# Slot tables by one-hot products instead of scatters, and a new order of splits, gathers and loads

## The chip, the cores and the metric

The kernel runs on one core of a Trainium2 chip. The metric is device time of one execution in microseconds (us). The engines are TensorE (PE; its weight loads are listed as PEld), VectorE (DVE), ScalarE (ACT), GpSimd (POOL) and SyncE (SP), which issues most DMA transfers. Each engine runs its own instructions in order.

## The reference

Three stages follow one another on 4 batches of 1152 positions, 8 heads of 64.

1. Attention: queries are averaged in pairs (576 per batch); scores against all 1152 keys, softmax, product with V. Its output, transposed, is x: 2304 rows of 512.
2. A routed expert layer: rows with `x @ w_skip > 0` go to the best of 8 experts by `x @ w_gate`, are sent through `relu(xc @ w1[e]) @ w2[e]`, scaled by the gate's probability and added to x. The other rows pass unchanged.
3. A dense layer on all rows: `((x @ w1) * (x @ w2)) @ w3 @ w_out`, with 512 to 1024 to 1024 to 512 columns.

```python
skip_score = x @ w_skip
do_compute = skip_score > 0
e_idx = np.argmax(logits, axis=1)
h = np.maximum(xc[mask] @ w1[e], 0.0)
y[mask] = gate_w[mask, None] * (h @ w2[e])
out[do_compute] = xc + y
...
h = a * b @ w3
return (h @ w_out).astype(np.float32)
```

The weights of stage 3 arrive as 64-bit floats and are converted to 32 bits on the chip.

## The kernel before

Matrix products in fp32 are made of pieces of type fp32r: a value is split into a high and a low part (names end in h and l), and three products of the parts are added. Splitting is work for ACT (the high part, a cast) and DVE or POOL (the low part, a subtraction).

**Attention** is a loop over 144 steps (16 head pairs, `p`, of 9 query tiles, `l`) and 7 more to drain it. Its order is written by hand: in step `i` PE transposes the exponentials of step i-2 (L289), multiplies some of them with V (L325) and makes the scores of step i (L255). DVE takes the maximum (L266) and a third of the copies out of PSUM, ACT the exponentials and the other copies (L308). POOL prepares the K and Q of later head pairs (`prep`, L208, L209, in two phases of steps) from raw buffers that SP loads. Beside this, two generators are advanced by `side`:

- `conv_ops` converts the stage-3 weights in 40 chunks: SP loads a chunk, POOL squares its high words (L82), DVE makes four operations of it (L96, L97, L101, L104), SP stores it to DRAM (L105). It is advanced from step 8 on.
- `route_ops` runs once per batch, 44 steps after the batch's first: logits, the choice of expert, and the position of each row among the rows of its expert (products with a triangle of ones). Ten indirect DMAs of POOL (`put`, L417) then scatter the row numbers into two tables in DRAM: `tab` (rows ordered by expert) and `perm` (skipped rows in front, then the others). Its letters say what comes next: "P" is PE work, which `side` does only in steps where a PSUM bank is free, "D" is DVE work, "C" the scatters. At the end it transposes five blocks of x (L448), scales them into the row buffers `XR` (L451; four buffers, block 4 uses buffer 0 again) and has SP store them to `x_d` in DRAM (L456).

**Transition.** The last batch's route runs after attention. As a filler for PE, the product W' = w3 @ w_out is made in eight blocks of 24 matmuls (`wprime`, L513). Its operand, the third weight, comes in blocks of 128 columns (`RW`, two buffers) and is split by ACT (L554), DVE and POOL (L555, L556). `emit_meta` computes on one partition which expert each tile of 128 rows has. Then SP loads the order vector and three index columns from DRAM (L823, L587) and the first expert's weights, POOL gathers rows from `x_d` (`gather`, `ld_x`), and `split` splits the weights.

**Expert loop.** Up to 25 tiles of 128 rows, each in a runtime `If` nested in the one before; 11 run with these inputs. Each tile: `xg @ W1`, relu, transposes, `@ W2`, and a scatter of the rows back to `x_d`. When the expert changes, weights are split and the next ones loaded.

**Dense stage.** Six groups of 384 rows, fetched by the order vector: products with m1 and m2 (L883), their product, and the product with W' (L513). Its first steps split m1 and m2 into the buffers of the expert weights (`split_cols`, L865, L866).

## Time and profile before

| | |
|---|---|
| median of 3 runs | 1099.67 us (1098.1 to 1102.2) |
| profiled execution | 1107.73 us, span of its records 1105.6 us |
| mean granted clock of PE | 0.981 |
| busy share of the span | PE 93%, PEld 76%, DVE 53%, ACT 44%, POOL 36% |
| DMA | 144.92 MB |

Attention takes about half of the span, the transition from there to 632 us, the expert loop to 777 us, the dense stage the rest. Times in rows are microseconds from the start of the span. A busy PE means that its matmul records cover the time; granted clock 1.00 is 2.4 GHz, 0.50 is 1.2 GHz.

### The profile page before, as it was taken

To read this page: it belongs to the slowest core of one execution; us is meant where nothing else is said; L and a number is where in the kernel's file an instruction comes from. 1 tells how busy PE (TensorE), PEld (TensorE's weight loads), DVE (VectorE), ACT (ScalarE), POOL (GpSimd) and SP (SyncE) were. 2 spreads that over 40 slices of the span, in tenths; PEclk is the share of its full clock that TensorE was granted. 3 is DMA by queue.
4 is the path that set the end of the run, shared out by engine and by line. 5 is a ranking of instruction groups with operands and counts; after the bars stand their busy time and mean duration, and the time that the engine had idled before them with its cause. 6 is when DMAs were issued, how large, how long until landed. Compare 5 with 4: busy or idle time off the path is not lost. (4 is left out here: it accounts for less than half of the span.)

```text
span 1105.6 us, 16864 instructions
## 1 busy us (share of the span) xinstructions
PE 1031.4 (93%) x6060; PEld 834.8 (76%) x6060; DVE 583.6 (53%) x883; ACT 482.3 (44%) x903; POOL 393.7 (36%) x411
## 2 busy tenths in 40 slices
PE   5799999999999899899998699998899999999995
PEld 4577776777767677676776488786799898989894
DVE  6588888788876788775633322437531221213120
ACT  4466665666655566565521322434432221212120
POOL 4643524563544435250824623439301010110101
PEclk9899999999999999999999699999899999999998
DMA  9776787587874878527518841506101010100000
GB/s 265 193 229 195 225 234 219 117 192 218 250 223 89 186 212 251 151 66 150 163 39 125 265 168 40 188 24 240 34 10 48 14 44 20 39 33 26 29 1 31
DMA packets 73003, 144.92 MB, mean 131 GB/s; under 512 B 16576, under 2 KB 26304, under 8 KB 72898
## 3 DMA queue, kind: packets, MB, share of 16 engines
q1 hardware_dynamic: 63698, 127.79, 41.7%
q0 software_dynamic: 6080, 14.26, 4.0%
q10 hardware_dynamic: 3120, 1.57, 0.9%
q8 instruction: 53, 0.87, 0.4%
q14 instruction: 52, 0.43, 0.1%
HBM read 86.23 MB, written 22.96 MB: 99 GB/s over the span
## 5 line engine op out<-in xcount | busy, mean ns | idle before, releaser
L266 DVE TENSOR_REDUCE sm<-s 128x1 f32<-128x1152 f32 x144 | 195.3, 1356 | 117.5 <-PE s L255 91.5
L255 PE MATMUL s<-k,q 128*128 128x384 f32 x864 | 204.9, 364 | 29.4 <-DVE pt L308 17.3
L255 PEld LDWEIGHTS s<-k,q 128*128 128x128 f32 x864 | 147.2, 192 | 98.1 <-issue 46.9
L308 ACT COPY pt<-s 128x384 f32<-128x384 f32 x288 | 137.6, 479 | 179.9 <-PE s L289 173.9
L278 ACT ACTIVATE p<-s,sm 128x1152 f32<-128x1152 f32 x144 | 176.3, 1224 | 16.6 <-DVE sm L266 16.1
L325 PE MATMUL vb<-pt,vr 128*64 128x256 f32 (+1 forms) x1152 | 170.7, 418 | 4.3 <-DVE xr L451 2.5
L289 PE MATMUL s<-cs,p 128*128 128x128 f32 x1296 | 169.7, 277 | 4.0 <-ACT p L278 3.6
L289 PEld LDWEIGHTS s<-cs,p 128*128 128x128 f32 x1296 | 151.2, 143 | 14.8 <-ACT p L278 7.5
L887 DVE TENSOR_TENSOR ar<-b,ar 128x384 f32<-128x384 f32 x48 | 26.7, 557 | 189.7 <-PE b L883 189.7
L902 POOL DMA_INDIRECT out_dram<-ar,ord x18 | 17.9, 994 | 271.0 <-ACT ar L901 266.3
L325 PEld LDWEIGHTS vb<-pt,vr 128*64 128x64 f32 x1152 | 70.2, 136 | 56.7 <-issue 22.5
L308 DVE COPY pt<-s 128x384 f32<-128x384 f32 x144 | 78.8, 547 | 2.7 <-PE s L289 1.8
L209 POOL TENSOR_TENSOR kl<-kr,kh 128x384 fp32r<-128x384 f32 x45 | 47.5, 1056 | 77.2 <-DMA k<-kl 66.6
L888 ACT CAST CVh<-ar 128x384 fp32r<-128x384 f32 x48 | 24.6, 513 | 107.7 <-DVE ar L887 107.7
L82 POOL TENSOR_TENSOR cm<-ch 128x512 f32<-128x512 f32 x40 | 42.1, 1057 | 76.1 <-DVE ca L104 47.1
L513 PE MATMUL b<-W1h,CVh 128*128 128x512 f32 x176 | 60.1, 402 | 0.7 <-issue 0.5
L513 PE MATMUL b<-W2h,CVh 128*128 128x512 f32 x176 | 60.7, 404 | 0.2
L513 PE MATMUL b<-WPh,CVh 128*128 128x512 f32 x144 | 57.4, 399 | 0.0
L513 PE MATMUL b<-WPl,CVh 128*128 128x512 f32 x144 | 56.9, 395 | 0.0
L513 PE MATMUL b<-WPh,CVl 128*128 128x512 f32 x144 | 56.8, 394 | 0.0
L901 ACT COPY ar<-b 128x512 f32<-128x512 f32 x18 | 10.6, 587 | 86.2 <-PE b L513 86.2
L208 POOL TENSOR_SCALAR kh<-kr 128x384 fp32r<-128x384 f32 x45 | 26.3, 584 | 57.9 <-PE s L255 52.1
(194 smaller groups left out, 1799.0 us busy)
## 6 DMA issues: line engine op xcount, KB each, us to landing
R<-in_w_dram SPq DMA_DIRECT2D x16, 1024.0 KB, 8.8
vr<-in_v_dram SPq DMA_DIRECT2D x16, 576.0 KB, 4.9
kr<-in_k_dram SPq DMA_DIRECT2D x15, 576.0 KB, 5.3
qr<-in_q_dram SPq DMA_DIRECT2D x15, 576.0 KB
k<-kh SPq DMA_DIRECT2D x30, 288.0 KB, 5.7
k<-kl SPq DMA_DIRECT2D x30, 288.0 KB, 15.3
q<-qnl SPq DMA_DIRECT2D x60, 144.0 KB, 4.2
ch<-in_w3t_dram SPq DMA_DIRECT2D x16, 512.0 KB, 4.8
```

Source lines behind the costliest of these rows:

```text
L82: POOL.tensor_tensor(m, hf, hf, op=ALU.mult)
L208: POOL.tensor_scalar(KH[i][:, cc], rawk[p][:, cc], 1.0, 0.0, op0=ALU.mult, op1=ALU.add)
L209: POOL.tensor_tensor(KL[:, cc], rawk[p][:, cc], f(KH[i][:, cc]), op=ALU.subtract)
L255: m = PE.matmul(sp[:, c, 0:384], lhsT=lt, rhs=kk[:, 384 * c:384 * c + 384], start=(n == 0), stop=(n == len(seq) - 1))
L266: DVE.tensor_reduce(sm, sp[:, :, 0:384], axis=AX.XY, op=ALU.max, negate=True)
L278: ACT.activation(pt, sp[:, :, 0:384], AF.Exp, bias=sm, scale=1.0, accum_out=SM[b][:, hp, c:c + 1])
L289: m = PE.transpose(tp[:, u * 128:u * 128 + 128], src[:, kt * 128:kt * 128 + 128], ident)
L308: m = (DVE.tensor_copy(o, i_) if eng is DVE else ACT.copy(o, i_)).ins
L325: PE.matmul(acc[64 * h:64 * h + 64, 0:n], lhsT=vr[:, h, kt, :], rhs=pt[:, kt, h, :], start=(kt == 0), stop=(kt == KT - 1))
L513: PE.matmul(o, lhsT=lh[a], rhs=rh[b_], start=(first and n == 0), stop=(last and n == len(order) - 1))
L887: DVE.tensor_tensor(cv, pb[:, 0:GT], av, op=ALU.mult)
L888: ACT.copy(CV[0][:, c], cv)
```

## The change

- **Tables in SBUF.** The scatters and the DRAM tables go. The index of a row is divided into a low part (7 bits, the partition of its slot) and a high part (the column). For each block of 128 rows two one-hot matrices are built by comparison with an `iota` row: 128 columns for the low part, and 146 (`tab`) plus 18 (`perm`) columns for the high part, these multiplied by row number plus one. A matmul of the two puts every row number into its slot, and DVE adds the result to `slots`. In the first three batches POOL builds, into two buffers, and the matmuls of each block are a "P" of their own; in the last batch DVE builds all five blocks, and ten matmuls in a row add them up. Empty slots are then set to an index out of bounds. The index column of a tile is copied from SBUF; the order vector needs no load.
- **Third weight.** The converted third weight is stored in blocks of columns, so that an `RW` block is one run of 4 KB in each partition; there are three `RW` buffers, loaded further ahead by SP, and DVE alone makes the low parts in `wprime`.
- **Buffers.** Five row buffers instead of four, one raw K buffer instead of two (the second raw K of the start uses `KL`), the temporaries of `emit_meta` in a part of `WPr`.
- **Order.** The conversion starts earlier: its first squares at step 4, its further steps from step 6. The index copies come before the first load of W1. `gather(1)` comes before `ld_x(0)`. The transposes of the first dense group (`x2_first`) move into tile 0, m2's load behind W2's next load. m1's split moves into the `Else` arm of each nested `If`, where it runs once, when the tiles have ended; m2's split stays behind the loop.

```diff
+    def c_src(name, c):
+        if name == "w3t":
+            return wsrc[name].rearrange("(a p f) t -> p a f t", p=128, f=F)[:, c % 8, CW * (c // 8):CW * (c // 8) + CW, :]
+        return wsrc[name].rearrange("(p n) t -> p n t", p=128)[:, c * CW:(c + 1) * CW, :]
+
+    def c_dst(name, c, t):
+        if name == "w3t":
+            u, a = 4 * (c // 8), c % 8
+            SP.dma_start(wd[name].rearrange("(u p a f) -> p u a f", u=8, p=128, f=128)[:, u:u + 4, a],
+                         t.rearrange("p (u f) -> p u f", u=4))
+        else:
+            SP.dma_start(wd[name].rearrange("(p n) -> p n", p=128)[:, c * CW:(c + 1) * CW], t)
...
         ms = [sq(nxt[0]), sq(nxt[1])]
+        yield
...
-    XR = [keep.tile([128, XW], F32, name=f"xr{i}") for i in range(4)]
+    XR = [keep.tile([128, XW], F32, name=f"xr{i}") for i in range(5)]
...
+        OB = [mid.tile([128, 256 + NSL + NCNT], F32R, name=f"ob{i}") for i in range(2)]
...
-            rawk[p] = erl.tile([128, S], F32, tag="kr", name="kr", bufs=2)
+            rawk[p] = erl.tile([128, S], F32, tag="kr", name="kr", bufs=1)
...
-            sp_ = keep.tile([128, NTT, 1], I32, tag="sp", name="sp")
-            DVE.tensor_tensor(sp_, tp_, pb[:, :, NE:NE + 1], op=ALU.add)
-            scat = {id(tab): [], id(perm): []}
-
-            def put(t, ix, j, top):
-                m = POOL.indirect_dma_start(
-                    out=t[:, :], out_offset=bass.IndirectOffsetOnAxis(ap=ix[:, j, :], axis=0),
-                    in_=idt[:, b, j:j + 1], in_offset=None, bounds_check=top, oob_is_err=False).ins
-                for e in scat[id(t)]:
-                    tc.declare_no_dep(m, e, reason="other slots")
-                scat[id(t)].append(m)
...
+            DVE.tensor_tensor(si[:, 1].unsqueeze(2), tp_, pb[:, :, NE:NE + 1], op=ALU.add)
+            hl = keep.tile([128, 2, 2, NTT], I32, tag="hl", name="hl", bufs=1)
+            DVE.tensor_scalar(hl[:, 0], si, 127, None, op0=ALU.bitwise_and)
+            DVE.tensor_scalar(hl[:, 1], si, 7, None, op0=ALU.logical_shift_right)
+            hf_ = keep.tile([128, 2, 2, NTT], F32, tag="hf", name="hf", bufs=1)
+            DVE.tensor_copy(hf_, hl)
+            E = DVE if hook else POOL
+            ob = {}
...
+            def build(j):
+                t = ob[j] = obs[j % len(obs)]
+                for u in range(2):
+                    E.tensor_scalar(t[:, 128 * u:128 * u + 128], iota[:, 0:128], hf_[:, 0, u, j:j + 1], None,
+                                    op0=ALU.is_equal)
+                for u, c0, n in ((0, 256, NSL), (1, 256 + NSL, NCNT)):
+                    E.tensor_scalar(t[:, c0:c0 + n], iota[:, 0:n], hf_[:, 1, u, j:j + 1], idf[:, b, j:j + 1],
+                                    op0=ALU.is_equal, op1=ALU.mult)
+
+            parts = ((0, 0, NSL), (1, NSL, NCNT))
+            for j in range(len(obs)):
+                build(j)
+            if len(obs) == NTT:
+                yield "P"
+                tp = tbank()
+                for u, c0, n in parts:
+                    for j in range(NTT):
+                        t = ob[j]
+                        PE.matmul(tp[:, c0:c0 + n], lhsT=t[:, 128 * u:128 * u + 128], rhs=t[:, 256 + c0:256 + c0 + n],
+                                  start=(j == 0), stop=(j == NTT - 1))
+                DVE.tensor_tensor(slots, tp[:, 0:NSL + NCNT], slots, op=ALU.add)
             else:
                 for j in range(NTT):
-                    put(tab, si, j, SLOTS - 1)
-                    put(perm, sp_, j, N - 1)
-                    yield "C"
+                    yield "P"
+                    tp = tbank()
+                    t = ob.pop(j)
+                    for u, c0, n in parts:
+                        PE.matmul(tp[:, c0:c0 + n], lhsT=t[:, 128 * u:128 * u + 128], rhs=t[:, 256 + c0:256 + c0 + n],
+                                  start=True, stop=True)
+                    DVE.tensor_tensor(slots, tp[:, 0:NSL + NCNT], slots, op=ALU.add)
+                    if j + len(obs) < NTT:
+                        build(j + len(obs))
             if hook:
-                hook()
+                fr_ = hook[1]
+                DVE.tensor_scalar(fr_, slots, 0.0, float(PADID + 1), op0=ALU.is_equal, op1=ALU.mult)
+                DVE.scalar_tensor_tensor(TAB, slots, -1.0, fr_, op0=ALU.add, op1=ALU.add)
+                hook[0]()
...
-                xr = XR[j % 4]
+                xr = XR[j]
...
-            if k != "D" and kinds != "P":
+            elif k != "D":
...
-            RW = [wp.tile([128, 8, 128], F32, name=f"RW{i}") for i in range(2)]
+            RW = [wp.tile([128, 8, 128], F32, name=f"RW{i}") for i in range(3)]
...
+            def ld_rw(u):
+                SP.dma_start(RW[u % 3], wd["w3t"].rearrange("(u p a f) -> u p a f", u=8, p=128, f=128)[u])
...
+            for u in range(3):
                 POOL.tensor_scalar(WS[u][0], RW[u], 1.0, 0.0, op0=ALU.mult, op1=ALU.add)
                 POOL.tensor_tensor(WS[u][1], RW[u], f(WS[u][0]), op=ALU.subtract)
+                ld_rw(u + 3)
...
-                    DVE.tensor_tensor(ws[1][:, 0:4], rw[:, 0:4], f(ws[0][:, 0:4]), op=ALU.subtract)
-                    POOL.tensor_tensor(ws[1][:, 4:8], rw[:, 4:8], f(ws[0][:, 4:8]), op=ALU.subtract)
-                if fc >= 1 and fc + 4 < 8:
-                    ACT.dma_start(RW[fc % 2], wv["w3"][:, :, 128 * (fc + 4):128 * (fc + 4) + 128])
-
+                    DVE.tensor_tensor(ws[1], rw, f(ws[0]), op=ALU.subtract)
+                if fc + 6 < 8:
+                    wv["ld"](fc + 6)
...
+        TAB = slots.bitcast(I32)
+        ORD = TAB[:, NSL:NSL + NCNT]
...
-            SP.dma_start(IDX[j % 5], tab[bass.ds(st, 128), :])
+            SP.dma_start(IDX[j % 5], TAB[:, bass.ds(st, 1)])
...
+            if j == 0:
+                x2_first()
...
-                        if g == 1 and i > 7:
-                            side("DC")
+                        if g == 1 and i > 5:
+                            side("D")
...
+                if i == 4:
+                    next(conv)
...
-                emit_meta()
+                emit_meta(WPr[0:1, 6:8].rearrange("p a f -> p (a f)"))
+                ld_idx(0)
+                ld_idx(1)
+                ld_idx(2)
...
-            SP.dma_start(ORD, perm.rearrange("(c p) o -> p (c o)", p=128))
-            ld_idx(0)
-            ld_idx(1)
-            ld_idx(2)
             gather(0)
+            gather(1)
             ld_x(0, XG)
-            gather(1)
...
+            SP.dma_start(R3, mview("m2"))
...
+            def split_m1():
+                for c in range(0, 8, 2):
+                    split_cols(W1, R1, c, c + 2)
+
+            def tiles(j):
+                with tc.If(T > j) as cmp:
+                    tile_body(j, x2_first)
+                    if j + 1 < NTILE:
+                        tiles(j + 1)
+                    else:
+                        split_m1()
+                with cmp.Else():
+                    if j == 0:
+                        x2_first()
+                    split_m1()
+            tiles(0)
...
-                split_cols(c0, c1)
+                split_cols(V2, R3, c0, c1)
```

## Rows read from the trace of the kernel before

**Rows 1.** The page, busy time: us, share of the span, instructions.
```profile
PE 1031.4 (93%) x6060; PEld 834.8 (76%) x6060; DVE 583.6 (53%) x883; ACT 482.3 (44%) x903; POOL 393.7 (36%) x411
```

**Rows 2.** PE's waits: total us, times, longest us.
```profile
PE s L255 <- DVE pt L308: 17.3, 11, 6.3
...
PE b L513 <- POOL WSl L556: 4.2, 1, 4.2
```

**Rows 3.** Timeline, 36 to 52 us: start, us, engine, line, operation, count, idle before.
```profile
44.47 1.51 DVE L96 SCALAR_TENSOR_TENSOR cm<-cm,ch 128x512 f32<-128x512 f32 x1 [6.48 <-POOL cm L82]
...
43.40 2.03 POOL L82 TENSOR_TENSOR cm<-ch 128x512 f32<-128x512 f32 x2
```

**Rows 4.** Stretches: busy us (instructions) per engine, granted clock, DMA share, GB/s.
```profile
46.00:50.00 4.00, 1.43 (x4) 1.35 (x5) 3.79 (x5) 1.31 (x2) 3.68 (x5) 0.50 0.01 2
...
100.00:200.00 100.00, 98.00 (x669) 71.96 (x669) 84.45 (x111) 65.61 (x123) 46.72 (x51) 1.00 0.81 225
...
560.10:604.10 44.00, 41.25 (x168) 30.72 (x168) 1.00 0.47 74
...
600.00:604.00 4.00, 4.00 (x18) 3.00 (x16) 0.00 (x0) 0.00 (x0) 0.00 (x0) 1.00 1.08 174
...
612.00:616.00 4.00, 2.93 (x7) 2.38 (x8) 2.64 (x5) 4.00 (x8) 0.44 (x1) 0.50 0.36 5
```

**Rows 5.** Timeline of the transition, 585 to 633 us.
```profile
588.10 22.17 SPq L456 DMA_DIRECT2D x_d<-xr  x5
...
609.01 0.68 DVE L451 TENSOR_TENSOR xr<-vb,r 64x512 f32<-64x512 f32 x1 [12.93 <-DMA x_d<-xr]
...
611.49 1.04 ACT L554 CAST WSh<-RW 128x1024 fp32r<-128x1024 f32 x1 [16.62 <-DMA RW<-w3t]
...
613.07 0.80 PE L513 MATMUL b<-CCh,WSh 128*128 128x512 f32 x1 [9.04 <-ACT WPr L552]
...
632.13 0.50 PE L513 MATMUL b<-W1h,CVh 128*128 128x512 f32 x1 [0.50 <-issue]
```

**Rows 6.** Timeline: first and last instruction of the metadata; a gather.
```profile
578.26 0.15 DVE L470 TENSOR_TENSOR nb<-base,cs 1x8 f32<-1x8 f32 x1
...
584.51 0.18 DVE L509 TENSOR_SCALAR meta<-ej 1x26 int32<-1x26 f32 x1
...
621.09 1.00 POOL L592 DMA_INDIRECT xr<-x_d,ix  x1 [0.30 <-issue]
```

**Rows 7.** Timeline of a route step in attention, 346 to 348 us.
```profile
346.89 1.01 POOL L417 DMA_INDIRECT tab<-idt,si x1 [11.93 <-DVE sp L413]
347.21 1.14 PE L289 MATMUL s<-cs,p 128*128 128x128 f32 x9
```

**Rows 8.** Single lines: durations in ns, least/median/most; first and last start; shapes.
```profile
L208 POOL TENSOR_SCALAR kh<-kr x45: 506/512/959, 21.7 to 473.6; 128x384 fp32r<-128x384 f32 x45
...
L188 DVE TENSOR_SCALAR ca<-ca x2: 294/294/295, 4.8 to 12.2; 128x256 f32<-128x256 f32 x2
...
L393 PE MATMUL vb<-oh,csr x20: 253/262/270, 206.7 to 575.4; 128*128 128x50 f32 x4, 128*128 128x40 f32 x4, 128*128 128x30 f32 x4, 128*128 128x20 f32 x4
...
L97 DVE TENSOR_SCALAR cm<-cm x40: 426/428/1518, 46.0 to 490.6; 128x512 int32<-128x512 int32 x40
```

**Rows 9.** The loop's end, 774 to 790 us: branch instructions, then the timeline.
```profile
L852 PEldq COMPARE_BRANCH  x2: 198/1804/3409, 776.3 to 780.1; - x2
...
780.17 0.62 ACT L865 CAST W1h<-R 128x512 fp32r<-128x512 f32 x1 [8.58 <-DVEq L852]
...
780.84 0.69 PE L883 MATMUL b<-X2h,W1h 128*128 128x384 f32 x1 [3.82 <-ACT W1h L865]
...
789.08 1.21 DVE L866 TENSOR_TENSOR W2l<-R,W2h 128x1024 fp32r<-128x1024 f32 x1
```

**Rows 10.** DMA issues: count, KB each, median us from issue to landing.
```profile
R<-in_w_dram SPq DMA_DIRECT2D x16, 1024.0 KB, 8.8
...
x_d<-xr SPq DMA_DIRECT2D x16, 258.0 KB, 3.1
```

More of the change, by code (lines that the diff above doesn't have):

```diff
@@ L29 @@
 NJ = NTILE + 1
+NSL = NE * NCNT + 2
 CW = 512
@@ L151, in load_first @@
                 rawq[0, h] = erl.tile([128, 2, SQ], F32, tag="qr", name="qr", bufs=2)
[L152 removed]
+                rawk[0, h] = f(KL) if h else erl.tile([128, S], F32, tag="kr", name="kr", bufs=1)
             def lq(h, c0, c1):
@@ L406, in route_ops @@
             DVE.scalar_tensor_tensor(po, cm, -float(PADID), po, op0=ALU.mult, op1=ALU.add)
-            si = keep.tile([128, NTT, 1], I32, tag="si", name="si")
-            DVE.tensor_scalar(si, po, float(PADID), None, op0=ALU.add)
+            si = keep.tile([128, 2, NTT], I32, tag="si", name="si")
+            DVE.tensor_scalar(si[:, 0].unsqueeze(2), po, float(PADID), None, op0=ALU.add)
             tp_ = keep.tile([128, NTT, 1], F32, tag="tp", name="tp")
@@ L506, in emit_meta @@
             DVE.tensor_copy(meta[:, :, 3], ej)
-            DVE.tensor_scalar(ej, ej, float(N), None, op0=ALU.mult)
-            DVE.scalar_tensor_tensor(ej, df2, 128.0, ej, op0=ALU.mult, op1=ALU.add)
-            DVE.tensor_scalar(meta[:, :, 1], ej, float(SLOTS), None, op0=ALU.min)
+            DVE.scalar_tensor_tensor(ej, ej, float(NCNT), df2, op0=ALU.mult, op1=ALU.add)
+            DVE.tensor_scalar(meta[:, :, 1], ej, float(NSL - 1), None, op0=ALU.min)
         def mm3(o, lh, rh, first, last, order=((0, 0), (0, 1), (1, 0))):
@@ L538, in wprime_fill @@
                     yield
-            POOL.tensor_scalar(WS[2][0], RW[0], 1.0, 0.0, op0=ALU.mult, op1=ALU.add)
-            POOL.tensor_tensor(WS[2][1], RW[0], f(WS[2][0]), op=ALU.subtract)
-            yield
-            SP.dma_start(RW[0], wv["w3"][:, :, 512:640])
         def wprime(B, WP):
@@ L704, in body @@
             SP.dma_start(idt, ids)
-            DVE.memset(padt, PADID)
+            DVE.memset(slots, 0.0)
             DVE.memset(lgp, 0.0)
@@ L774, in body @@
                         DVE.tensor_copy(csr, cs[:, C_U:C_U + 256])
+                    if i == 2:
+                        PE.matmul(VB[1][:, 0:128], lhsT=ones, rhs=tri, start=True, stop=True)
+                        DVE.tensor_copy(iota[:, 0:128], VB[1][:, 0:128])
+                        DVE.tensor_scalar(iota[:, 128:NSL], iota[:, 0:NSL - 128], 128.0, None, op0=ALU.add)
+                        DVE.tensor_scalar(idf, idt, 1.0, None, op0=ALU.add)
                 if l in (8, 0, 1, 3, 4, 5) and rts.get("k") == "P":
@@ L845, in body, with x2_first, split_cols @@
             xpose(0)
-            for t in range(NTG):
-                x2t(X2a, t, XG[t])
+            def x2_first():
+                for t in range(NTG):
+                    x2t(X2a, t, XG[t])
             split(W2, R2, 8)
             ld_next(R2, w2, 0)
+            SP.dma_start(R3, mview("m2"))
             T = nc.values_load(mT[0:1, 0:1], min_val=0, max_val=NTILE)
             ns = nc.values_load(mT[0:1, 2:3], min_val=0, max_val=N)
-            with ExitStack() as st:
-                for j in range(NTILE):
-                    st.enter_context(tc.If(T > j))
-                    tile_body(j)
+            def split_cols(W, r, c0, c1):
+                cols = slice(128 * c0, 128 * c1)
+                ACT.copy(W[0][:, :, cols], r[:, :, cols])
+                DVE.tensor_tensor(W[1][:, :, cols], r[:, :, cols], f(W[0][:, :, cols]), op=ALU.subtract)
+            def split_m1():
[13 more added lines that the diff above has]
+            tiles(0)
             V2 = [W2[x].rearrange("p a f -> p (a f)").rearrange("p (a f) -> p a f", a=4) for x in range(2)]
@@ L861, in body @@
             OT = [a1[:, D * i:D * i + D] for i in range(2)]
-            def split_cols(c0, c1):
-                cols = slice(128 * c0, 128 * c1)
-                for W, r in ((W1, R1), (V2, R3)):
-                    ACT.copy(W[0][:, :, cols], r[:, :, cols])
-                    DVE.tensor_tensor(W[1][:, :, cols], r[:, :, cols], f(W[0][:, :, cols]), op=ALU.subtract)
             for c0, c1 in ((0, 1), (1, 2), (2, 4), (4, 6), (6, 8)):
-                split_cols(c0, c1)
+                split_cols(V2, R3, c0, c1)
             rctx.close()
```

75 lines of the change are left out of this document (38 added, 37 removed).

## The prediction

> **What bounds the kernel now.** I read the page's busy line first: TensorE (PE) is busy for 93% of the span, no other engine above 53% [rows 1]. So only time in which PE stands still, or runs at half clock, can be won, and every matmul added in a stretch that PE fills is lost. The list of PE's waits shows where it stands still [rows 2]; the timelines show on what.
>
> The longest wait on a VectorE (DVE) copy, 6.3 us, is at the start. DVE did nothing for 6.5 us because its first conversion step (L96) stood behind GpSimd's (POOL's) squares L82, and POOL reached those only at 43.40, after a head pair's preparation [rows 3]. Behind the wait PE ran at half clock: 46 to 50 us shows 0.50 [rows 4].
>
> The larger loss lies between attention and the expert loop. W' is a filler of 192 matmuls; 168 had run by 604, lastly 18 in 4 us [rows 4], and 24 were left, 5.4 us. But PE stopped at 604 and resumed at 613.07 [rows 5], then stopped again for 4.2 us for POOL's half of a split [rows 2]. Two things were late together. ACT's cast L554 waited 16.6 us for an RW block of the third weight, which is read in runs of 512 bytes. DVE waited 12.9 us at L451, because row block 4 reuses row buffer 0, whose store was unfinished: SP spent 22 us on those five stores, behind W1's load [rows 5]. The stretch 612 to 616, at clock 0.50, moved 5 GB/s, when the order vector was loaded from DRAM word by word [rows 4]. The first expert matmul started at 632.13 [rows 5]. After that PE is nearly always full, up to a stop of 3.8 us at the loop's end [rows 9].
>
> **The change part by part.** All times are in the profiled execution's own clock: span 1105.6, its own time 1107.7.
>
> *Start.* One more yield and a call at step 4 put the first two squares on POOL before the preparation of step 6, so DVE's first conversion, now in step 6, finds them done. That removes 6.3 us, and about 4 us of PE work behind it no longer runs at half clock, 2 us. DVE may wait 1 us for the squares, as POOL ends an earlier preparation just before. Sum -7.5; bounds 0 (the wait only moves) and -9. One raw-K buffer instead of two costs nothing as long as POOL consumes a pair before its successor is loaded, as the code's steps have it; if that cover goes, SP's queue waits, and the K, Q and conversion loads behind it are late. The iota product, the memset and the float ids are under 1 us of work on engines that wait at that point.
>
> *One-hot products in attention.* For three batches, ten scatters per batch (about 1 us each, on POOL) are replaced by five builds of four POOL operations and five pairs of PE matmuls, each pair with a DVE addition. Scatters had no PE instruction behind them; the products have all of attention behind them. POOL is free when the indices are ready: it had waited 11.9 us for them [rows 7]. The first pair is emitted in the very step that computes the indices. There DVE has three more small operations, 0.6 us, so POOL starts at about 347.2. A POOL tensor_scalar of 384 columns takes 0.51 us [rows 8]; 128 to 146 columns should be near 0.3, 18 near 0.2, so a build takes some 1.36 us with its gaps. PE started its next transposes at 347.21 [rows 7]; it now gets operands at about 348.8. I count 1.85 us for the first stall and pair, and 0.3 us for each of the four others, built a step ahead; small matmuls start 0.11 us apart and take 0.26 each [rows 8]. That is 3.05 us a batch, 9.2 for three, and 1 us for 15 additions on DVE, busy 84% here [rows 4]. I take +10. The lower bound is 30 matmuls at 0.11, +3.4, with POOL's builds hidden; the upper one is the third rival's.
>
> POOL's builds read and write SBUF beside DVE, and the trace shows what that can cost: L97, the same 512 columns forty times, takes 0.43 us at the least and the median, 1.52 at the most [rows 8]. The Trainium skill, "SBUF — State Buffer", section "Who interferes with whom", says that POOL and a DVE operation in a two-port mode exclude each other for the whole instruction. By that rule a build could hold DVE for its whole length; by the median row it costs nothing.
>
> *Between attention and the loop.* The last route builds on DVE: 20 operations; 256 columns take 0.29 us [rows 8], and as independent ones overlap I take 2.5 us: indices at 578.7, builds done at 581.3. PE has three pieces of W' in front (until 579.7) and then ten small matmuls: PE is 2.3 us later. Table and metadata follow; the metadata took 6.4 us, 578.26 to 584.69 [rows 6], and now runs from 582.9 to 589.3. The three index copies, ahead of W1's load, take SP some 3 us, so W1 is issued near 593.5. A half landed 8.8 us after its issue [rows 10]; the row blocks' stores follow, the last issued at 600. No scatters and no RW blocks share the engines, so all are down near 606.5. A gather is 1.0 us and 0.3 of issue [rows 6]: five end at 613, and the first rows are there by 610. The third weight comes a product ahead into three buffers, in 4 KB runs, and DVE splits it alone: neither of PE's two stops remains. The filler ends at 609.4 + 2.3 + 0.5 = 612.2, the transposes of tile 0 and their split follow, its first matmul comes at 613.7: -18.4. The transposes of the first group of skipped rows move into tile 0, +2.9 there, and POOL's last chunk of W1 is at the limit, +1. Sum -14.5. Bounds: -18.4, if tile 0 hides what moved into it, and -9, if W1's load and the stores still take 22 us: rows at 615.5, POOL's part of W1 six later.
>
> The third weight's stores become four runs of 512 bytes per partition. They lie in attention, on a queue that waits for DVE's conversion anyway; I count nothing, 2 us at most. The fifth row buffer only removes the wait at L451. m2's load moves behind W2's next load; it is needed at the loop's end. But SP's index copy for tile 3 stands behind both: it should land near 645, and its gather is due by 649.
>
> *Loop's end.* m1's split moves into an Else arm, before the engines join. ACT, idle for 8.6 us before 780.17 [rows 9], can do it in that time. But PE's own far branch took 3.41 us [rows 9], which fills the stop by itself, and stays. PE then leaves through eleven nested joins, each a short branch. DVE is free at about 780 and does four halves of m1, 1.21 us each [rows 9]; PE waits for all of them where it waited for one column block. What ACT gains and what PE waits about cancel. I take +1; bounds -3 and +4.
>
> The Trainium skill, "Runtime: NRT & Kernel Launch", section "Instruction fetch mechanics", says that a taken branch to code outside the loaded pages waits for a fetch. The trace agrees: the other branch of that row took 0.2 us. A second fetch on the way out would be 3.4 us more, by the same row, which the upper bound holds.
>
> Sum: -7.5 + 10 - 14.5 + 1 = -11, so 1096.7 in the profiled execution's time. That execution lies 8.06 us above the median of the runs, 1099.67; with the same difference the median becomes 1088.7. **Forecast 1089 us.**
>
> **The rivals** (in median time).
>
> 1. *The transition keeps a large part of its loss*, by the slow W1 load above: -9 in place of -14.5, 1094; if tile 3's gather is late too, by some 4 us, 1098. For it: the SP queue takes everything in order, and the metadata comes 4.6 us later than before. Against: scatters and RW blocks shared the engines then. Chance 0.18.
> 2. *The products are hidden.* PE pays 3.4 instead of 10: 1082. Against it: the first pair comes in the same step as its indices. Chance 0.12.
> 3. *Slower: the builds hold DVE.* Place: the 15 builds in attention. DVE idles 16% there [rows 4], about half a microsecond of a step, so what a lock takes, PE mostly loses. A whole build is 1.36 us, 15 are 20.4: 1109. It decides (above 1105.2) from 1.1 us a build. For it: L97's maximum, 1.1 us above its minimum. Against it: L97's median, though POOL was busy for 47% of the stage [rows 4]; and much of a build falls beside the maximum over the scores, which reads PSUM. Chance 0.10.
> 4. *The start keeps its wait*, because the chunk loads or POOL are late at step 4: 1096. Chance 0.07.
>
> **How the numbers follow.** 0.5%, 5.5 us, is about what a measurement of this kernel can tell from no change; so faster means below 1094.2. The forecast, own range 1082 to 1094, has 0.53; with the hidden products and a part of the first rival (0.05), faster is 0.70. Same is the rest of the first rival and the fourth, 0.20. Slower is 0.10. The range goes from 1078 (products hidden, start and transition near their best) to 1101, which leaves out the lock at its full price.
>
> **What the profile after would show.** Right: no idle DVE near 38 to 44 us and no half clock near 46; one-hot matmuls behind a PE wait of about 1.5 us, once in each of three batches; no PE gap over 2 us between the filler's start and its end; the first expert matmul near 616 (613.7, less 7.5, plus 10); the stop at the loop's end still there. Wrong: PE waits for POOL at most pairs, DVE conversion at double length beside builds, W1 and the stores taking 22 us, or PE waiting for the first gather or tile 3's. The forecast stands or falls with the size of two terms, +10 and -14.5.

## The result, and the profile after

The kernel after the change takes 1090.1 us (median; 1085.9 to 1092.7), against 1100.9 for the kernel before in the same series: a ratio of 0.990, 95% interval 0.985 to 0.994. The forecast was 1089 in a range of 1078 to 1101. The number fits. Its sum does not: one cost was put too high, one gain was put too high, and one gain was missing.

To see that, I place marks in the two profiles: the start of the last maximum of attention, the transposes that begin the third tile of the expert loop (by then everything that moved within the transition has been paid for), the first dense matmul, the last scatter of the output, and the end of the span.

| start of ..., us | before | after | lead |
|---|---|---|---|
| maximum of step 16 | 75.3 | 69.2 | 6.1 |
| maximum of step 48, ahead of the first products | 189.4 | 184.3 | 5.1 |
| last maximum of attention | 551.2 | 549.5 | 1.7 |
| transposes of the third tile | 650.7 | 640.8 | 9.9 |
| first dense matmul | 780.8 | 771.8 | 9.0 |
| last scatter of the output | 1093.8 | 1083.4 | 10.5 |
| end of the span | 1105.6 | 1090.8 | 14.8 |

So the start gave 6.1; from there to the end of attention 4.4 were lost; the transition gave 8.2; loop's end and dense stage together gave 0.6; and 4.3 came behind the last scatter, where the prediction had nothing.

The list of PE's waits after (engine, line, what it waited for: total us, times, longest us):

```profile
PE s L271 <- DVE k L197: 7.8, 2, 6.6
PE s L271 <- DVE pt L324: 7.5, 11, 1.2
PE vb L465 <- POOL ob L444: 5.9, 3, 2.0
PE b L952 <- DVE W1l L913: 4.7, 1, 4.7
...
PE vb L456 <- DVE R L444: 1.8, 4, 0.5
PE b L560 <- POOL W1l L684: 1.7, 2, 0.9
```

The first line is old: it took 7.7 us before, too. The wait of 6.3 us at the start [rows 2] is gone from the second line: its longest is now 1.2. The waits of 9.0 and 4.2 for the third weight's copy and split [rows 2, 5] are gone altogether. New are the third line, one stop of 2.0 us in each of the three batches, and the first behind the cut, at the ten products of the last batch.

Stretches after (busy us and instructions for PE, PEld, DVE, ACT, POOL; granted clock; DMA share; GB/s):

```profile
46.00:50.00 4.00, 4.00 (x31) 2.79 (x27) 3.25 (x5) 3.19 (x8) 3.60 (x6) 1.00 1.01 413
206.00:216.00 10.00, 7.92 (x43) 5.39 (x42) 5.68 (x14) 4.82 (x10) 6.83 (x11) 0.83 0.00 1
582.00:590.00 8.00, 8.00 (x28) 6.51 (x29) 6.60 (x29) 0.00 (x0) 0.00 (x0) 0.67 0.01 2
612.00:616.00 4.00, 3.27 (x17) 2.56 (x16) 1.69 (x4) 1.75 (x4) 3.20 (x3) 1.00 0.73 213
```

The first and last answer to the same stretches of before, at clock 0.50 [rows 4]; both now run at 1.00. The two between are where PE loses: at the first pair of a batch and behind the last batch's products, PE first stands still and then runs at a lower clock.

The first pair of the first batch in the timeline after (start, us, engine, line; in brackets the idle time before it and what ended it):

```profile
209.17 1.21 POOL L441 TENSOR_SCALAR ob<-iota,hf 128x128 fp32r<-128x128 f32 x2 [7.51 <-DVE hf L434]
...
210.37 1.29 POOL L444 TENSOR_SCALAR ob<-iota,hf,idf 128x146 fp32r<-128x146 f32 x2
...
211.29 0.75 PE L465 MATMUL vb<-ob 128*128 128x146 f32 x2 [1.99 <-POOL ob L444]
...
211.90 2.18 PE L305 MATMUL s<-cs,p 128*128 128x128 f32 x9
```

POOL's four operations take 2.5 us, not 1.36. PE waits 1.99, makes the pair in 0.6, and the nine transposes behind it take 2.18 where the same nine took 1.14 [rows 7]. From step 52 to step 56 the lead falls from 5.1 to 0.8 us: 4.3 us for one pair that came too early.

### The profile page after: what moved, and what is told of

Its sections match the earlier page's. It is cut to its first block, busy times and chain, and to the rows that moved or that the text cites. A ratio compares the mean times of both kernels' runs of the same rounds, so it can differ in the third digit from the quotient of the medians.

```text
span 1090.8 us, 16927 instructions
## 1 busy us (share of the span) xinstructions
PE 1038.4 (95%) x6101; PEld 839.9 (77%) x6101; DVE 598.0 (55%) x934; ACT 482.4 (44%) x902; POOL 387.0 (35%) x426
## 5 line engine op out<-in xcount | busy, mean ns | idle before, releaser
L341 PE MATMUL vb<-pt,vr 128*64 128x256 f32 (+1 forms) x1152 | 173.9, 422 | 4.5 <-DVE xr L490 2.1
L305 PE MATMUL s<-cs,p 128*128 128x128 f32 x1296 | 172.0, 279 | 2.9 <-ACT p L294 2.9
L971 POOL DMA_INDIRECT out_dram<-ar,slots x18 | 18.1, 1003 | 272.1 <-ACT ar L970 267.4
```

The costliest lines, as they stand in the source:

```text
L305: m = PE.transpose(tp[:, u * 128:u * 128 + 128], src[:, kt * 128:kt * 128 + 128], ident)
L341: PE.matmul(acc[64 * h:64 * h + 64, 0:n], lhsT=vr[:, h, kt, :], rhs=pt[:, kt, h, :], start=(kt == 0), stop=(kt == KT - 1))
```

## The experiments

Each kernel is the changed one with the edit shown. Medians of separate series differ by a few us for the same kernel (the kernel before gave 1098.7 to 1105.0), and the five kernels whose attention is that of the changed one (it, 4, 5, 7 and 9) end it anywhere from 544.8 to 549.5 us, 547.1 in the mean. Kernels 6, 10 and 12 also store the third weight in the old way during attention and end it at 543.5 to 544.8; that the new stores cost some 3 us there is suggested by this, not shown. So effects are read between marks, not only from medians. The lower ratios of 5 and 7 show no gain by themselves: in their series the kernel before was at its slowest, 1105.0, and the changed kernel was not run. The marks (us; "third tile" is counted from the last maximum of attention, the tail from the start of the last scatter to the end of the span):

| kernel | last maximum | third tile behind it | POOL's indirect DMAs | tail | span | median, ratio to before |
|---|---|---|---|---|---|---|
| before | 551.2 | 99.5 | 100 | 11.8 | 1105.6 | |
| after | 549.5 | 91.2 | 60 | 7.4 | 1090.8 | 1090.1, 0.990 |
| 1 later pair | 531.9 | 90.3 | 60 | 7.4 | 1075.3 | 1076.7, 0.979 |
| 2 scatters, three batches | 561.0 | 90.3 | 90 | 10.5 | 1105.3 | 1104.7, 1.005 |
| 3 old start | 553.5 | 89.8 | 60 | 7.4 | 1093.4 | 1095.2, 0.997 |
| 4 filler moved | 546.7 | 90.9 | 60 | 7.4 | 1087.7 | 1088.7, 0.990 |
| 5 four row buffers | 544.8 | 90.7 | 60 | 7.4 | 1086.4 | 1085.0, 0.981 |
| 6 old third weight | 543.9 | 91.1 | 60 | 7.4 | 1083.4 | 1089.0, 0.987 |
| 7 m1 behind the loop | 548.4 | 90.9 | 60 | 7.4 | 1087.0 | 1086.6, 0.983 |
| 8 stores first | 532.6 | 88.5 | 60 | 7.4 | 1072.5 | 1074.0, 0.971 |
| 9 scatters, last batch | 546.3 | 91.5 | 70 | 8.9 | 1090.2 | 1092.1, 0.990 |
| 10 both (6 and 9) | 543.5 | 103.1 | 70 | 8.7 | 1098.1 | 1100.4, 0.998 |
| 11 as 8, m1 behind | 533.4 | 88.1 | 60 | 7.4 | 1071.2 | 1072.6, 0.972 |
| 12 scatters, old layout | 544.8 | 92.8 | 70 | 8.9 | 1090.6 | 1091.7, 0.992 |

**1. The first pair one step later.**

```diff
             else:
+                yield "D"
                 for j in range(NTT):
                     yield "P"
```

> Against the changed kernel (own time 1092.7, median 1090.1). Theory: what the products cost in attention is the first pair of each batch, which PE reaches while POOL is still building (stops of 1.97 to 2.0 us, then half clock). One step later the builds of about 2.5 us are done: no PE wait for POOL at the first pair, no half clock behind it, 3 to 4 us less per batch, attention ends 8 to 11 us earlier, median 1080 to 1083. Rival: the cost lies in the pairs themselves (two weight loads, an addition on DVE, POOL kept from the conversion's squares and the head pairs), so it only moves: attention ends less than 3 us earlier, median 1087 to 1090.

Attention ends 17.7 us before that of the changed kernel, 15.3 before the mean of the five. The stretch with the first pair, and the list of waits, which no longer names POOL's one-hot matrices at all, show why:

```profile
206.00:216.00 10.00, 10.00 (x73) 7.77 (x71) 7.64 (x16) 6.98 (x14) 7.27 (x12) 1.00 0.00 1
```

PE is full, at clock 1.00, with 73 instructions in place of 43. All pairs are still made and added, and POOL builds as slowly as before. The mechanism of the theory holds, and the price was higher than it said: from the step ahead of a first pair to the one behind it, this kernel gains 4.3 to 5.6 us on the changed one in each batch.

**2. Scatters back in three batches**, behind the fifth pair, into unread tables.

```diff
+                for j in range(NTT):
+                    put(tab, 0, j, NE * N - 1)
+                    put(perm, 1, j, N - 1)
```

> The changed kernel with the ten scatters of each of the first three batches put back behind the fifth pair, into tables that nothing reads. Theory: scatters were not free in the kernel before. POOL is held for 12 to 13 us per batch and the small packets delay loads: attention ends 3 to 8 us later than in the changed kernel; and the last wait of POOL at the program's end grows with the number of indirect DMAs (100 of them: 8.24 us, 60: 4.98), so with 90 it is 7.4 us, and the semaphore step before it 2.0 in place of 1.39: the tail behind the last scatter of the output takes 10.5 us in place of 7.4. Median 1096 to 1101. Rival: scatters are off PE's path, as the prediction had it, and the tail's length has another cause: attention within 1.5 us, tail 7.4 us, median 1089 to 1092.

Attention ends 11.4 us later than in the changed kernel and 13.8 later than the mean of the five, more than the theory said. The DMA view of 372 to 400 us, first the changed kernel, then this one (by queue, packets, MB and share of the engines' time; q0 are POOL's; below, transfers with count, KB and median us to landing):

```profile
q1 hardware_dynamic: 2048, 5.42, 59.4%
...
x_d<-xr SPq DMA_DIRECT2D x4, 258.0 KB, 3.2
```

```profile
q1 hardware_dynamic: 1635, 4.15, 87.0%
q0 software_dynamic: 320, 0.01, 0.9%
...
x_d<-xr SPq DMA_DIRECT2D x4, 258.0 KB, 14.2
...
kr<-in_k_dram SPq DMA_DIRECT2D x1, 576.0 KB, 11.0
qr<-in_q_dram SPq DMA_DIRECT2D x1, 576.0 KB, 17.2
```

The scatters' own packets fill 0.9% of the engines' time, but the other queue takes 87% in place of 59% for fewer bytes, and its transfers take several times as long. The largest loss behind them is one stop of PE:

```profile
403.94 0.24 POOL L240 TENSOR_SCALAR bd<-qnl 64x64 fp32r<-64x64 f32 x1 [12.97 <-DMA m<-ca]
...
405.34 1.51 DVE L113 SCALAR_TENSOR_TENSOR cm<-cm,ch 128x512 f32<-128x512 f32 x1 [5.91 <-POOL cm L98]
...
409.99 1.33 PE L343 MATMUL vb<-pt,vr 128*64 128x320 f32 x4 [7.49 <-issue]
```

POOL stands 13.0 us. By the profile it waits for a store of the conversion, issued at 388.22; the last of its own scatters, issued at 387.47, had landed only 0.3 us before that wait ended. So the scatters hold up POOL by their own landing as well as by the store's, and this run does not separate the two. DVE then waits for POOL's squares, and PE starts again behind DVE's late work; for this last link the profile names no releaser. The stop of 7.5 us is over half of the loss.

The kernel before shows transfers as slow as these: beside the second batch's scatters, 347 to 361 us, transfers of K took 14.0 us, and at 379.60 PE had stood 2.04 us for one of Q.

The tail was forecast to a tenth: 10.5 us. What grows is, for 3.3 of the 4.3 us between before and after, a DRAIN of POOL behind the program's last line; the step INC_SWDGE_SEM ahead of it went from 2.20 to 1.39 us (durations in ns: least/median/most; after, this kernel, before):

```profile
L1041 POOLq DRAIN  x3: 46/107/4975, 1085.0 to 1090.5; - x3
```

```profile
L1056 POOLq DRAIN  x3: 46/111/7425, 1097.0 to 1105.0; - x3
```

```profile
L972 POOLq DRAIN  x3: 46/111/8242, 1096.5 to 1105.3; - x3
```

60, 90 and 100 indirect DMAs give 4.98, 7.43 and 8.24 us, and 70 in experiment 9 give 5.79: 0.082 us for each that the program has issued, however long ago.

**3. The old start of the conversion.**

```diff
-        yield
...
-                        if g == 1 and i > 5:
+                        if g == 1 and i > 7:
...
-                if i == 4:
-                    next(conv)
```

> The changed kernel with the conversion's start as it was before. Theory: the early start is worth what the first steps show, 6 us: the maximum of step 16 comes 5.5 to 7.5 us later than in the changed kernel, and the end of attention too, median 1095 to 1098. Rival: the steps behind have slack that takes the gain back (the lead of 6.1 us at step 16 was 3.8 at step 28): attention ends less than 3 us later, median 1090 to 1093.

The maximum of step 16 comes at 75.7 in place of 69.2, as before the change, and attention ends 3.9 us after the changed kernel's, 6.3 after the mean of the five. At step 16 the theory holds. At the end of attention the gain survives by more than the rival says; against the changed kernel it is less than the theory says, against the mean it is as forecast.

**4. Twelve filler matmuls ahead of the last batch's products.**

```diff
-            pieces = {0: 1, 2: 1, 4: 3, 5: 3}
+            pieces = {0: 1, 2: 1, 4: 3, 5: 5}
...
-            fill(9)
+            fill(7)
```

> The changed kernel with 12 of the filler's matmuls moved from behind the last batch's products to in front of them. Theory: the transition missed its forecast because PE reaches the ten products while DVE still builds (1.84 us of stops between 578 and 581) and then runs 11 matmuls of W' at half clock (2.2 us): both go, the filler ends 3 to 4 us earlier and the third tile starts 2 to 4 us earlier; median 1086 to 1088. Rival: the row blocks' stores and POOL's share of W1, which queues behind five gathers, set the start of the loop: the third tile starts at most 1 us earlier, and PE's waits for POOL at W1 grow by what the filler gains; median 1089 to 1091.

Half of the theory holds: from 574 to 590 PE is full at clock 1.00. But the third tile stays where it was (90.9). The timeline shows where the time went:

```profile
613.05 1.09 PE L689 MATMUL b<-cs,xr 128*128 128x128 f32 x4 [6.83 <-DMA xr<-x_d,ix]
```

PE had run out of filler at 606.2 and waited for the first gather, issued at 606.5 behind the last row store, which had taken 9.3 us to landing. The rival holds: stores and gather set the start of the loop.

**5. Four row buffers.**

```diff
-    XR = [keep.tile([128, XW], F32, name=f"xr{i}") for i in range(5)]
+    XR = [keep.tile([128, XW], F32, name=f"xr{i}") for i in range(4)]
...
-                xr = XR[j]
+                xr = XR[j % 4]
```

> The changed kernel with four row buffers, block 4 in buffer 0 as before. Theory: the last batch's block 4 waits again on DVE for the store of block 0, whose transfer shares the queues with W1 (8.9 us to landing), so the last store is issued 3 to 5 us later; the first gather waits for that store (it does so in the kernel with the moved filler), and the filler's cover is used up: the third tile starts 2 to 5 us later than the 91 us behind the end of attention; median 1092 to 1095. Rival: another transfer or POOL's share of W1 sets the start of the loop, and the wait on DVE is hidden: third tile within 1 us, median 1089 to 1091.

Third tile at 90.7: the theory falls, the fifth buffer is worth nothing here.

**6. The old third weight**: stored row by row, two buffers, half of the split on POOL (cut).

```diff
-                SP.dma_start(RW[u % 3], wd["w3t"].rearrange("(u p a f) -> u p a f", u=8, p=128, f=128)[u])
+                SP.dma_start(RW[u], wv["w3"][:, :, 128 * u:128 * u + 128])
...
-                    DVE.tensor_tensor(ws[1], rw, f(ws[0]), op=ALU.subtract)
-                if fc + 6 < 8:
-                    wv["ld"](fc + 6)
+                    DVE.tensor_tensor(ws[1][:, 0:4], rw[:, 0:4], f(ws[0][:, 0:4]), op=ALU.subtract)
+                    POOL.tensor_tensor(ws[1][:, 4:8], rw[:, 4:8], f(ws[0][:, 4:8]), op=ALU.subtract)
+                if fc >= 1 and fc + 4 < 8:
+                    ACT.dma_start(RW[fc % 2], wv["w3"][:, :, 128 * (fc + 4):128 * (fc + 4) + 128])
```

> The changed kernel with the third weight as before: stored row by row, read in runs of 512 bytes into two buffers on ACT's queue, low parts half on POOL. Theory: without scatters beside them the blocks come in time, but POOL's halves stand behind its gathers and the loads share the queues with W1 and the row stores: PE stops again between 595 and 620, 3 to 6 us, and the third tile starts 3 to 6 us later relative to the end of attention; median 1093 to 1096. Rival 1: the third weight alone was what stopped PE before, and all of its 13 us come back: median 1100 to 1103. Rival 2: only the scatters had made it late: within 1 us, median 1089 to 1091.

Third tile at 91.1: theory and first rival fall. By itself this part of the change moved nothing. (The lower span comes from elsewhere: from the third to the last transposes the loop took 113.5 us in place of 117.4. The edit does not explain this, as kernel 10, which has it too, took 117.3.)

**7. m1's split behind the loop.**

```diff
-                with cmp.Else():
-                    if j == 0:
-                        x2_first()
-                    split_m1()
+                if j == 0:
+                    with cmp.Else():
+                        x2_first()
...
             for c0, c1 in ((0, 1), (1, 2), (2, 4), (4, 6), (6, 8)):
+                split_cols(W1, R1, c0, c1)
                 split_cols(V2, R3, c0, c1)
```

> The changed kernel with m1's split back behind the loop, in five steps between those of m2. Theory: the split in the Else arm wins nothing, because PE's far branch of 3.4 to 3.7 us fills the stop and DVE has a far branch of its own (2.8 us) ahead of its first quarter: the stop from the last expert matmul to the first dense one is 3.8 us again in place of 4.7, and the first dense group ends 0 to 1 us earlier; median 1089 to 1091. Rival: the Else arm hides ACT's casts, and without it the first column blocks are late: the stop grows to 6 us or more and the dense stage starts 2 to 3 us later; median 1092 to 1094.

The first dense matmul here:

```profile
767.27 0.69 PE L950 MATMUL b<-X2h,W1h 128*128 128x384 f32 x1 [3.91 <-ACT W1h L912]
```

and in the changed kernel:

```profile
771.82 0.66 PE L952 MATMUL b<-X2h,W1h 128*128 128x384 f32 x1 [4.71 <-DVE W1l L913]
```

The stop is 0.8 us shorter without that part of the change, and what it waits for is again ACT, as before [rows 9]. The other kernels bear this out: the stop is 3.8 to 3.9 us in the three without the Else arm's split (before, 7 and 11) and 4.7 to 5.5 in the eleven with it. But nothing of it is left at the end: from the start of the stop to the last scatter of the output, both this kernel and the changed one take 316 us.

**8. Experiments 1 and 4, and the row stores ahead of W1's load.**

```diff
                 ld_idx(2)
-                ld_w(R1, w1, 0, 3)
...
+            ld_w(R1, w1, 0, 3)
             gather(0)
```

> The changed kernel with the first pair one step later, the 12 filler matmuls moved, and W1's load issued behind the five row stores. Attention as with the later pair alone (end 17.7 us before the changed kernel's). Theory for the rest: with the filler moved the loop's start hangs on the last row store (9.4 us to landing beside W1 and W2) and the gather behind it (6.3 us); with the stores in front they land in 4 to 6 us, the first tile's transposes start at 60 to 63 us behind the end of attention in place of 65 to 66, the third tile 85 to 88 in place of 90 to 91; median 1071 to 1075. Rival: the bytes are the same and W1 is then as late as the rows were: the third tile at 90 or more, median 1076 to 1079.

The first tile's transposes start 60.1 us behind the end of attention in place of 64.9, but the third tile only at 88.5. PE's first W1 product waits:

```profile
592.74 0.63 PE L690 MATMUL b<-cs,xr 128*128 128x128 f32 x4 [0.27 <-issue]
595.73 0.50 PE L561 MATMUL b<-W1h,CVh 128*128 128x512 f32 x1 [2.36 <-ACT CVh L692]
```

The cast that it needs stands on ACT behind the casts of W1, and those waited for W1's load. So theory and rival both have a part: about half of the gain of the rows is given back at W1.

**9. The last batch's scatters alone**, behind its builds, into unread tables.

```diff
+            if hook:
+                for t, u, top in ((tab, 0, NE * N - 1), (perm, 1, N - 1)):
+                    for j in range(NTT):
+                        m = POOL.indirect_dma_start(
+                            out=t[:, :], out_offset=bass.IndirectOffsetOnAxis(ap=si[:, u, j:j + 1], axis=0),
...
```

> The changed kernel with the ten scatters of the last batch alone put back, at their old place, into tables that nothing reads. Neither the four row buffers nor the old third weight moved the transition, so what took 8 to 9 us there is open. Theory: the scatters' small packets, as in attention, where a row store beside them took 14.2 us to landing in place of 3.2: W1, the row stores and the first gather come late, and the third tile starts 4 to 9 us later behind the end of attention (95 to 100 in place of 89.8 to 91.2); the tail, with 70 indirect DMAs, is 8.5 us. Median 1093 to 1099. Rival: the scatters are over before W1 and the stores begin, and the gain came from the order of loads and gathers and the order vector that needs no load: third tile within 1.5 us, median 1087 to 1091.

Third tile at 91.5: the theory falls. Then neither the scatters nor the third weight nor the row buffer accounts for the transition by itself.

**10. Scatters and old third weight together** (the edits of 6 and 9).

> Both together: the last batch's ten scatters and the old third weight (which alone moved the transition by less than 0.3 us). Theory: the stop of 9 us before 613 in the kernel before came from the blocks of the third weight being read beside the scatters' packets, so together they cost 3 us or more above the scatters alone, and PE waits again for the cast of a block; third tile at 99 to 104 behind the end of attention. Rival: they do not add, within 1.5 us of the scatters alone.

Third tile at 103.1, 12 us above either alone. PE's list of waits, and the timeline of ACT and POOL:

```profile
PE b L565 <- ACT WPr L605: 6.5, 1, 6.5
```

```profile
572.27 0.37 ACTq L611 DMA_DIRECT2D RW<-w3t  x1
...
590.17 1.05 ACT L607 CAST WSh<-RW 128x1024 fp32r<-128x1024 f32 x1 [5.38 <-DMA RW<-w3t]
590.24 0.97 POOL L449 DMA_INDIRECT perm<-idt,si  x1 [8.30 <-DMA tab<-idt,si]
591.22 2.56 POOL L609 TENSOR_TENSOR WSl<-RW,WSh 128x512 fp32r<-128x512 f32 x2
...
592.57 0.37 ACTq L611 DMA_DIRECT2D RW<-w3t  x1
...
608.71 1.04 ACT L607 CAST WSh<-RW 128x1024 fp32r<-128x1024 f32 x1 [15.15 <-DMA RW<-w3t]
```

This is the picture of before: a cast that waits 16.6 us for a block, and behind it PE's stop of 9.0 [rows 5]. The forecast time came true, the theory's mechanism only in part. A block was read beside the scatters, the one asked for at 572.27, and it came only for the cast at 590.17. The block that took 16.1 us was not. It was asked for at 592.57, behind POOL's halves of the split, for POOL had stood 8.3 us until an earlier scatter had landed; and W1's load had gone out ahead of it, at 590.86. This is what the DMA engines did while it was on its way, 592.57 to 608.71 (packets, MB, share of the engines' time):

```profile
q1 hardware_dynamic: 1473, 2.86, 77.8%
q10 hardware_dynamic: 1040, 0.52, 12.1%
q0 software_dynamic: 32, 0.00, 0.1%
```

Of POOL's packets (q0) there were 32; q1 is SP's queue, with W1 and the row stores, and q10 is the block. So the scatters made the request late, and W1 and the stores made the transfer long. The kernel before has the same order: last scatter at 591.55, POOL's half at 592.53, the request at 593.87, W1's second half out at 588.06.

**11. Experiment 8 with m1's split behind the loop** (the edits of 7 and 8).

> The later first pair, the moved filler, the stores ahead of W1, and m1's split behind the loop. By the runs so far the last edit takes 0.5 to 1 us off the loop's end (stop of 3.9 in place of 4.7 to 5.0 us): median 1072 to 1074. Rival: it only moves the wait to m1's later columns: 1074 to 1076.

The stop at the loop's end is 3.9 us. At 1072.6 us, ratio 0.972 (0.967 to 0.978), it cannot be told from experiment 8 (0.967 to 0.974); both beat the kernel before and the changed one.

**12. Scatters, and only the layout of the old third weight** (experiment 9's edit, the old stores as in 6, and this).

```diff
-                SP.dma_start(RW[u % 3], wd["w3t"].rearrange("(u p a f) -> u p a f", u=8, p=128, f=128)[u])
+                SP.dma_start(RW[u % 3], wd["w3t"].rearrange("(a p f) -> p a f", p=128, f=F)[:, :, 128 * u:128 * u + 128])
```

> The scatters of the last batch, and of the old third weight only its layout: read in runs of 512 bytes, but into three buffers, loaded early by SP and split by DVE as in the changed kernel. The scatters with the whole old third weight cost 12 us; this separates why. Theory: it is the overlap. With three buffers the last two blocks are asked for before the scatters begin (565.6 and 571.6 against 574 in the kernel with the scatters alone), with two buffers one was asked for at 592.6 and took 16.1 us: here the third tile stays within 2 us of the scatters alone (91.5 behind the end of attention), median 1088 to 1094. Rival: it is the runs of 512 bytes, which the scatters' packets hold up whenever they are in flight: third tile at 97 or more, median 1095 to 1101.

Third tile at 92.8: the theory holds, and the layout is not the cause. The block of 564.13, in runs of 512 bytes, lands in 3.8 us, and the last is asked for at 570.16, ahead of the first scatter at 571.50. That requests ahead of the scatters are what counts fits this, and experiment 10. What makes them late there, two buffers, ACT's queue or POOL's half of the split, the runs do not choose: the three go together.

## Why the prediction came out right

*Start, -7.5.* Right in place, and near in size. DVE's first conversion waits 1.1 us for the squares, as said, and 46 to 50 us runs at 1.00. Measured 6.1 at step 16, and 3.9 to 6.3 at the end of attention (experiment 3).

*Products in attention, +10.* The net was +4.4, and both halves of it were wrong. The step "POOL starts at about 347.2", builds in 1.36 us, failed by its size: 128 columns take 0.60 us and 146 take 0.86, although 384 columns of another operation take 0.51 [rows 8], so a build is 2.5 us. The stop of 2.0 then came out near the 1.85 that I had counted for stop and pair, but the slow stretch behind it was not in the sum; the three first pairs alone cost some 14 us (experiment 1). And "scatters had no PE instruction behind them" failed: put back, they cost 13.8 us, by slow transfers and by POOL's wait for them (experiment 2). That the kernel before paid as much is not measured by itself, but the sum fits: 6.3 from the start and 13.8 less 15.3 make 4.8 us, and the five kernels end attention 4.1 before the kernel before. The 0.7 left for the other pairs, the additions and the third weight's stores is within the spread of those kernels.

*Transition, -14.5.* Measured 8.2, just outside the poor bound of 9. Of the 6.3 us that are missing, 3.7 were missing at the first expert matmul (615.74; counted from the end of attention 14.7 us earlier than before, where 18.4 were forecast) and 2.6 in the first two tiles (from there to the third tile's transposes 6.5 us longer, where 3.9 were counted). So the sign "first expert matmul near 616" came true by luck: attention had given 1.7 us where the sum had it lose 2.5. Two steps failed. "PE is 2.3 us later" for the ten products: it was 4.4 (578.03 to 582.46), with four waits for DVE, and eleven matmuls behind them at 0.43 us apart in place of 0.23 cost 2.2 more. Removing both won nothing (experiment 4), because of the second step, "five end at 613, and the first rows are there by 610". In the timeline of POOL after, the gathers run late and W1's last chunks behind them:

```profile
609.24 1.23 POOL L639 DMA_INDIRECT xr<-x_d,ix  x1 [56.77 <-issue]
...
616.33 1.16 POOL L683 TENSOR_SCALAR W1h<-R 128x512 fp32r<-128x512 f32 x1
...
623.00 1.27 POOL L684 TENSOR_TENSOR W1l<-R,W1h 128x512 fp32r<-128x512 f32 x1
```

W1 and W2 shared the DMA engines with the row stores in place of the scatters. The reason that I gave for the gain, scatters and RW blocks off the engines, was right, but as a pair: either one gone is enough (experiments 6, 9 and 10). Undone together they cost 12 us, more than the 8.2 that the transition gained; kernel 10 still has the ten products and the slow matmuls behind them (4.4 and 2.2 us), which the kernel before has not. What the new order of loads and gathers and the order vector that needs no load give was not separated. I had counted the fifth row buffer for its 12.9 us wait, and it was worth nothing (experiment 5).

*Loop's end, +1.* Right: the stop grew by 0.9 us. PE's far branch stayed, 3.67 us, and DVE's way into the Else arm ends only at 770.45, when PE was nearly back. The Trainium skill, "Runtime: NRT & Kernel Launch", section "Instruction fetch mechanics", was cited for a fetch at taken branches; these two agree with it. The dense stage behind it took 1.4 us less than before, so nothing of this is left at the last scatter.

*What was missing.* The sum went by the span and the profiled execution's own time and never asked what lies inside them behind the last matmul: 4.3 us of POOL's tail for 40 indirect DMAs.

*The step to the median.* By its own clock the change gave 14.8 us, not 11. The difference of 8.06 us between profile and median was carried over unchanged; it was 6.8 against the median of all runs of before, and 2.5 after (1092.7 against 1090.1). That is 4 to 6 us the other way. So the number rests on errors that cancel, in attention, in the transition, in the tail, and here.

*The rivals.* The first is what happened in the transition, by another cause: not the wait for W1's load of 22 us, but row stores, gather and POOL's queue. The second and fourth did not come. Of the third, POOL holding DVE, the same 512 columns as in [rows 8] show nothing,

```profile
L112 DVE TENSOR_SCALAR cm<-cm x40: 426/428/1533, 34.5 to 453.4; 128x512 int32<-128x512 int32 x40
```

but only one of these forty lies beside a build (it took 0.47 us). The lock shows elsewhere, the other way round, at DVE's conversion operations with two inputs:

```profile
487.67 0.68 DVE L119 SCALAR_TENSOR_TENSOR ca<-ch,cm 128x512 int32<-128x512 int32 x1
487.73 1.67 POOL L441 TENSOR_SCALAR ob<-iota,hf 128x128 fp32r<-128x128 f32 x2
```

Of the 60 POOL operations of the builds, the eight that begin while such an operation runs take 0.79 to 1.12 us in place of 0.43 or 0.60; the other 52 stay within 3% of the median of their kind. DVE's operations beside them keep 0.68 to 0.74. The Trainium skill, "SBUF — State Buffer", section "Who interferes with whom", says that the order of issue decides who waits. The eight agree: DVE was first, and POOL paid. Where a build was first, DVE's operation lost 0.06 us at most, so that a build holds DVE for its length is not seen here.

## What to carry to other kernels

Before work is put into a full engine's stream, ask in which step its operands are ready, and put it one step behind: the same products cost 14 us or almost none. Price what is removed too, by what its packets do to the transfers beside it, and count the indirect DMAs of the whole program for its end. When two causes meet in one stop, undo them singly and together; each alone showed nothing here, and together 12 us.

## What the runs showed of the hardware that had not been expected

- Scatters of 4 bytes per row slow other queues far beyond their own share: 320 packets, 0.9% of the engines' time, and row stores beside them took 14.2 us in place of 3.2 (median). The Trainium skill, "DMA: Bandwidth & Descriptors", section "Why small descriptors are slow (HBM only)", puts the cost of small descriptors into a fixed overhead on each of them; here the large transfers beside them pay, and why stays open.
- POOL's DRAIN at the end takes 0.082 us for each indirect DMA issued in the whole program (60, 70, 90, 100: 4.98, 5.79, 7.43, 8.24 us).
- POOL compares 128 columns with a value per partition in 0.60 us and 146, with a second operand, in 0.86; it multiplies 384 in 0.51. DVE took 0.28 for the 128. Width alone was no guide.
- A stop of 2.0 us cost more than itself: the nine transposes behind it took 2.18 us in place of 1.14, at a mean granted clock of 0.83 over the ten us around them.
